# Attention, a gated layer and a soft mixture of experts in one kernel: whole rows for the second matrices, a wider step in the catching-up, and routing in quarter steps

## The chip, the cores and the metric

The kernel runs on one core of a Trainium2 chip. The metric is the device time of one execution in microseconds (us), as the median of several runs. The engines of the core are named as in the profile: PE (TensorE, the matrix engine), DVE (VectorE), ACT (ScalarE), POOL (GpSimd) and SP (SyncE, which here only issues transfers). Data lie in DRAM, in SBUF (128 partitions) and in PSUM, the banks into which PE writes. Transfers go through 16 DMA engines.

## What is computed

Three layers follow each other; the sizes are 4 batches, 8 heads, 576 positions and 64 features per head, so 2304 tokens of 512 features.

```python
# 1: causal attention in a window of 64 positions
scores = scale * np.matmul(q, k.transpose(0, 1, 3, 2))
scores = np.where((rel >= 0) & (rel < 64), scores, -1e9)
x = softmax(scores) @ v                      # as [2304, 512]
# 2: gated layer, d_ff = 1536
x = (x @ w_a) * (x @ w_b) @ w_out            # [2304, 512]
# 3: soft mixture: 8 experts, 4 slots each, F = 1024
logits = x @ phi                             # [2304, 32]
d = softmax(logits, over the tokens)
slot_input = d.T @ x                         # [32, 512]
for e in range(8):
    slot_out[e] = np.maximum(slot_input[e] @ w1[e], 0) @ w2[e]
c = softmax(logits, over the slots)
out = c @ slot_out                           # [2304, 512]
```

The softmax over all tokens is what ties the stages together: no slot input is complete before the last token has been routed, and the experts' matrices (16 MB for w1 and w2 together) can be used only behind that.

## The kernel before

**Tiles and halves.** The tokens are worked in 18 tiles of 128. For each tile, attention gives x; the gated layer is cut into three groups of 512 hidden features (`fg`), and each group into a half `a` (x @ w_a) and a half `b` (x @ w_b), 12 matmuls each in PSUM (`psa`, `psb`, line 454). ScalarE copies psa out, and VectorE multiplies psb with it to g (line 463). These 108 half-blocks are the beat of the kernel. The matrix w_out is never multiplied with each token: its product with phi (`wphi`) makes the logits from g, and the weighted sums of g over the tokens (`ups` at line 600, kept in `acc`) are multiplied with w_out (`wo`) once, at the end.

**What happens between the halves.** A table `events` holds what is issued ahead of, or in the middle of, half-block n; `at(n, f, ...)` enters a step and `run_slot(n)` plays it. Attention steps of later tiles (`att_q`, `att_k`, `att_s`, `att_n`, `att_pt`, `att_pv`, and `load` for q, k, v) stand there, and the routing of earlier ones. Routing of a tile has these steps: `r_b` turns one group of g in 32x32 blocks on VectorE into gq, writes it to DRAM in four transfers `gd` and reads it back as gT in one (lines 486, 492, 497), all issued by SyncE; `r_ul` at half-block `R[t]` makes the sums of tile t-1 and the logits of tile t (`ups` at line 600 and at line 513, then `lt` at line 533 and the softmax); `r_k` and `r_d` follow. `R[t]` is 5 half-blocks behind the tile's last half, but at least 3 behind `R[t-1]`; the start of the kernel (the first five tiles' gated layer, half-blocks 0 to 29) goes without routing, so that from half-block 30 on the routing catches up, one tile every 3 half-blocks: tiles 2 to 9 at 37, 40, 43, 46, 49, 52, 58, 64. gT has four buffers in the pool p3. The queue of PE is the order of the code there (`manual_schedule`); on the other engines a scheduler orders.

**The last tiles.** The last three tiles (`LAST`) take PE to turn g (`r_t`: `tg`, line 138), and the table at the end of the events places their steps in half-block steps. Behind them come `tu` and `xs` (w_out with the sums, slot inputs), `sps`, and the experts: `h` with w1 (line 958), relu, transposes, then `ops` with w2 (line 992). `ops` is worked in two column halves n of 256 and two halves u of the experts (0 to 3, 4 to 7), each in eight steps m of 128 rows. Copies `o`, `so` (line 1010), `sor` (lines 1018 and 1019) prepare the slot outputs of a column half for `tokens_out(n, j)`: two matmuls `op` (line 1032) into a bank, a copy `ob` (line 1039) and a transfer of 256 KB to the output (line 1040). Nine such steps make a column half.

**Prefetching the matrices.** `order` lists the pieces that are wanted: 12 of wo, 64 of w1, 128 half pieces of w2 (`order2`: first all of column half 0, then of 1). `slots` lists the SBUF tiles that come free towards the end (of attention, x, g, and of w_a and w_b), and `fetch` issues for each freed slot as many pieces as it holds, on SyncE (line 748); a transfer waits on SyncE until the tile's last reader is done.

## Time and profile before

| | before |
|---|---|
| median of 3 runs | 518.61 us (518.32 to 519.11) |
| the profiled execution, its own time | 522.32 us |
| its span in the profile | 520.5 us |
| PE busy | 487.2 us, 94% |
| PE's share of the chain that ended last | 78% |
| DVE's share of that chain | 11% |
| moved by the DMA engines | 116.51 MB, mean 224 GB/s |

The span is what lies between the first and the last instruction; the profiled execution's own time has what lies around it. The profile's clock column is the granted share of PE's full clock: 1.00 is 2.4 GHz, 0.50 is 1.2 GHz. A wait in square brackets behind an instruction is idle time of its engine just before it, with what ended it; x is how many instructions a line puts together.

### The profile page before, as it was taken

To read this page: it belongs to the slowest core of one execution; us is meant where nothing else is said; L and a number is where in the kernel's file an instruction comes from. 1 tells how busy PE (TensorE), PEld (TensorE's weight loads), DVE (VectorE), ACT (ScalarE), POOL (GpSimd) and SP (SyncE) were. 2 spreads that over 40 slices of the span, in tenths; PEclk is the share of its full clock that TensorE was granted. 3 is DMA by queue.
4 is the path that set the end of the run, shared out by engine and by line. 5 is a ranking of instruction groups with operands and counts; after the bars stand their busy time and mean duration, and the time that the engine had idled before them with its cause. 6 is when DMAs were issued, how large, how long until landed. Compare 5 with 4: busy or idle time off the path is not lost.

```text
span 520.5 us, 10707 instructions
## 1 busy us (share of the span) xinstructions
PE 487.2 (94%) x4047; PEld 362.3 (70%) x4047; DVE 297.8 (57%) x765; ACT 195.9 (38%) x583; POOL 65.8 (13%) x136
## 2 busy tenths in 40 slices
PE   4769999999999999999899999999999999989993
PEld 2547786778778786877678788787877777743452
DVE  4997897889236757575546637467763210351222
ACT  4886675654314424242323324234432112241022
POOL 4100110100000111111202031131231000020000
PEclk9797999999999999999899999999999999999998
DMA  9999966642136877877885776667689999899997
GB/s 257 281 258 285 296 176 224 224 141 82 42 66 153 199 185 186 213 174 199 205 213 149 169 198 152 183 162 213 164 210 295 345 387 333 293 350 348 350 331 262
DMA packets 143715, 116.51 MB, mean 224 GB/s; under 512 B 81840, under 2 KB 124336, under 8 KB 143664
## 3 DMA queue, kind: packets, MB, share of 16 engines
...
## 4 chain that ended last, share of the span: by engine, by line
PE 78%; DVE 11%; DMA 7%; issue 1%; ACT 1%; SPq 0%; POOL 0%; POOLq 0%; ACTq 0%; DVEq 0%
PE psa L454 26%; PE psb L454 26%; PE xps L364 3%; DMA wo_dram<-wo 3%; PE ops L992 3%; PE s L273 3%; PE h L958 3%; PE ups L600 2%; PE ups L513 2%; PE tk L138 1%; PE tg L138 1%; DVE w L395 1%; DMA ldk<-in_k_dram 1%; PE tq L138 1%; DVE wo L395 1%
## 5 line engine op out<-in xcount | busy, mean ns | idle before, releaser
L454 PE MATMUL psa<-wa,x 128*128 128x512 f32 x648 | 167.3, 402 | 0.2 <-DVE wa L438 0.2
L454 PE MATMUL psb<-wb,x 128*128 128x512 f32 x648 | 165.2, 398 | 0.7 <-DVE wb L438 0.7
L454 PEld LDWEIGHTS psa<-wa,x 128*128 128x128 f32 x648 | 118.8, 190 | 28.0 <-issue 2.8
L454 PEld LDWEIGHTS psb<-wb,x 128*128 128x128 f32 x648 | 118.0, 188 | 26.7 <-issue 2.0
L463 DVE TENSOR_TENSOR g<-psb,g 128x512 f32<-128x512 f32 x53 | 36.5, 689 | 78.2 <-PE psb L454 69.3
L461 ACT COPY g<-psa 128x512 f32<-128x512 f32 x53 | 31.1, 587 | 94.0 <-PE psa L454 90.0
L293 ACT ACTIVATE pr<-pr,nmx 128x128 f32<-128x128 f32 x96 | 37.2, 389 | 17.1 <-DVE nmx L286 17.1
L330 POOL DMA_DIRECT2D pd<-pq x44 | 24.2, 557 | 102.2 <-DVE pq L323 73.8
L486 DVE STREAM_TRANSPOSE gq<-g 128x512 f32<-128x512 f32 x42 | 29.6, 706 | 0.7 <-DMA pd<-pq 0.4
L367 ACT CAST x<-xps 128x512 fp32r<-128x512 f32 x18 | 10.6, 586 | 44.8 <-PE xps L364 44.8
L314 DVE TENSOR_TENSOR pr<-pr,rs 128x512 f32<-128x512 f32 x36 | 24.4, 687 | 0.9
L273 PE MATMUL s<-kTs,qTs 64*64 64x128 f32 x576 | 21.8, 292 | 0.0
L236 POOL COPY kTs<-kTs 128x256 f32<-128x256 f32 x17 | 8.6, 506 | 103.7 <-DVE kTs L247 72.2
L336 POOL DMA_DIRECT2D pT<-pd x22 | 16.6, 757 | 39.2 <-DMA pd<-pq 31.8
L273 PEld LDWEIGHTS s<-kTs,qTs 64*64 64x64 f32 x576 | 17.1, 143 | 5.9 <-issue 4.5
L228 ACT ACTIVATE qTs<-tq 128x512 f32<-128x512 f32 x18 | 10.8, 599 | 26.6 <-PE tq L138 26.5
L138 PE MATMUL tq<-ident,ldq 128*128 128x128 f32 x72 | 11.9, 291 | 9.0 <-DMA ldq<-in_q_dram 7.9
L286 DVE CUSTOM_DVE_ANT_0 pr<-s,masks 128x128 f32<-128x128 f32 x80 | 17.5, 285 | 3.1 <-PE s L273 3.1
L293 ACT ACTIVATE pr<-s,nmx 128x128 f32<-128x128 f32 x48 | 17.1, 375 | 2.4 <-DVE nmx L283 2.4
L293 ACT ACTIVATION_READ_ACCUMULATOR pr<-pr,nmx 128x1 f32 x96 | 17.9, 187 | 0.0
L369 DVE TENSOR_TENSOR x<-xps,x 128x512 fp32r<-128x512 f32 x18 | 12.4, 690 | 8.7 <-ACT x L367 8.7
L549 ACT ACTIVATE e<-lt,nm 128x128 f32<-128x128 f32 x17 | 6.3, 369 | 29.5 <-DVE nm L545 29.4
...
## 6 DMA issues: line engine op xcount, KB each, us to landing
...
```

The source lines that it names most:

```text
L138: nc.tensor.transpose(o, i, ident)
L273: nc.tensor.matmul(sps[h][c, u], lhsT=qT[r, u, c], rhs=kTs[r, t % 2, u, W * b:W * b + P], start=not early, stop=not early or u == 3,)
L286: nc.vector.tensor_tensor_reduce(out=pr[:, u].rearrange("p (a k) -> p a k", a=2), in0=sps[h][:, u].rearrange("p (a k) -> p a k", a=2), in1 ...
L293: nc.scalar.activation(out=pr[:, u], in_=sps[h][:, u] if early else pr[:, u], func=ACTF.Exp, scale=-1.0, bias=nmx[:, i:i + 1], accum_out=s ...
L314: nc.vector.tensor_tensor(out=pr, in0=pr, in1=rs.to_broadcast([P, 4, P]), op=ALU.mult)
L330: nc.gpsimd.dma_start(out=pd[:, :, i].rearrange("j k e -> k j e"), in_=pq[32 * i:32 * i + 32].rearrange("p j h u q -> p j (h u q)"),)
L336: nc.gpsimd.dma_start(out=pT, in_=pd[:, :, :, P * h:P * h + P].rearrange("j k i e -> (j k) i e"))
L364: nc.tensor.matmul(o, lhsT=vt[:, 2 * u + h, :], rhs=r)
L454: nc.tensor.matmul(ps, lhsT=l[:, kk], rhs=r, start=(n == 0), stop=(n == 3 * KD - 1))
L461: nc.scalar.copy(out=pas[t, fg], in_=ps)
L463: nc.vector.tensor_tensor(out=g, in0=ps, in1=pas.pop((t, fg)), op=ALU.mult)
L486: nc.vector.transpose(out=gq.rearrange("p (j c t) -> p c j t", j=4, c=4), in_=gts[t][:, 512 * fg:512 * fg + 512].rearrange("p (c j f) -> p ...
```

## The change

1. **w2 in whole rows.** For experts 0 to 5 (`WHOLE = 6`) a piece of w2 is 128 whole rows of 512 columns, of which partition p holds rows 4p to 4p+3 of a block of 512 rows; neighbouring pieces that land in one slot go in one transfer, so that a partition's part of it is 2, 4 or 6 KB in one run (before: 1 KB runs of half rows). Such a piece is used in both column halves and is held until the second. Experts 6 and 7 stay in column halves. The order of loading is wo, w1 with two pieces of wo moved in among it, experts 0 to 3, experts 4 and 5, then experts 6 and 7 for column half 0 and for column half 1. The relu copies reorder h to match.
2. **Catching up.** `R[t]` is at least 4 behind `R[t-1]` for t from 3 on: tiles 2 to 9 at 37, 41, 45, 49, 53, 57, 61, 65; the `r_b` of a tile stand correspondingly earlier ahead of it. The pool's tag "e" becomes gq with four buffers and pq with one.
3. **Last tiles' routing.** The events table has quarter steps there; the last g is evacuated in two parts, the last transposes on ScalarE and VectorE, the last g is multiplied in two parts, the last tile's sums update acc in one instruction and not in three, the softmax over the slots of the last three tiles is one step, `both` and `turn_c` stand earlier, and the order on ScalarE and VectorE is that of the code from `tu` to the slot inputs.
4. **The end.** The first column half's nine `tokens_out` all stand within the second half's `ops`: four in u = 0, five in u = 1. Before, six stood in u = 0, one right behind u = 1's last `ops`, two behind `so`.

```diff
...
-    N_EX1 = 3
+    N_EX1 = 4
     N_EX2 = 6
-    EARLY = 6
-    PARTS = ((0, 256), (256, 256))
+    WHOLE = 6
+    EARLY = 4
+    HALF = DM // 2
...
-    wbufs = {"w0": 4, "w1": 4, "w2": 2, "w3": 2, "e": N_EX1}
+    wbufs = {"w0": 4, "w1": 4, "w2": 2, "w3": 2, "gq": N_EX1, "pq": 1}
...
-            nc.vector.tensor_tensor(out=g, in0=ps, in1=pas.pop((t, fg)), op=ALU.mult)
+            pa = pas.pop((t, fg))
+            step = 256 if (t, fg) == (NTILE - 1, NFG - 1) else 512
+            for c in range(0, 512, step):
+                nc.vector.tensor_tensor(out=g[:, c:c + step], in0=ps[:, c:c + step], in1=pa[:, c:c + step], op=ALU.mult)
...
+    def r_th(t, fg):
+        gT = pools["p3"].tile([P, 4, P], F32, tag=turn("gT"), name="gT", bufs=2)
+        for h in range(2):
+            tp = ps_t.tile([P, 2, P], F32, tag="t", name="tg")
+            for i in range(2):
+                f = 512 * fg + P * (2 * h + i)
+                transpose(tp[:, i], gts[t][:, f:f + P])
+            if h == 0:
+                nc.scalar.copy(out=gT[:, 0:2], in_=tp)
+            else:
+                nc.vector.tensor_copy(gT[:, 2:4], tp)
+        rst[t, fg] = gT
...
+        rsum = small.tile([P, NLAST], F32, tag="rsum", name="rsum")[:, 0:n]
+        for i in range(n):
+            nc.scalar.activation(
+                out=ce[:, i], in_=lk[:, NS * i:NS * i + NS], func=ACTF.Exp, bias=rm[:, i:i + 1], accum_out=rsum[:, i:i + 1]
+            )
...
+            nc.vector.tensor_tensor(out=cst[:, t:t + n], in0=ce, in1=rr.to_broadcast([P, n, NS]), op=ALU.mult)
...
-    slot_halves = {"g": 3, "as1": 1, "as2": 1, "gT1": 1, "w0": 4, "w1": 4, "w2": 4, "w3": 4}
...
-    order = [("o", c) for c in range(DFF // P)]
-    order += [("1", u, kk, e, n) for u in range(2) for kk in range(KD) for e in range(4) for n in range(2)]
-    order2 = [
-        ("2", n, u, mh, e)
-        for n, (_, nw) in enumerate(PARTS) for u in range(2) for mq in range(MF * nw // 1024)
-        for e in range(4) for mh in (2 * mq, 2 * mq + 1)
-    ]
-    order += order2
+    slot_halves = {"g": 3, "as1": 1, "as2": 1, "gT1": 1, "gq": 1, "w0": 4, "w1": 4, "w2": 4, "w3": 4}
+
+    order = [("o", 0, c) for c in range(DFF // P)]
+    order += [("1", (u, kk, e), n) for u in range(2) for kk in range(KD) for e in range(4) for n in range(2)]
+    for o, n in ((10, 25), (11, 28)):
+        order.insert(n, ("o", 0, o))
+        del order[order.index(("o", 0, o))]
+    order += [("r", (h, e), c) for h in range(2) for e in range(4) for c in range(4)]
+    order += [("r", (h, e), c) for h in range(2) for e in range(4, WHOLE) for c in range(4)]
+    order += [("c", (n, h, e), c) for n in range(2) for h in range(2) for e in range(WHOLE, NE) for c in range(4)]
...
+    def source(key, n):
+
+        kind, which, i = key
+        if kind == "o":
+            return wo_dram[P * i:P * (i + n)].rearrange("(c p) d -> p c d", p=P)
+        if kind == "1":
+            u, kk, e = which
+            return moe2_w1[4 * u + e][P * kk:P * kk + P, 512 * i:512 * (i + n)].rearrange("p (c d) -> p c d", d=512)
+        *n0, h, e = which
+        c = slice(HALF * n0[0], HALF * n0[0] + HALF) if n0 else slice(0, DM)
+        return moe2_w2[e][512 * h:512 * h + 512].rearrange("(p c) d -> p c d", c=4)[:, i:i + n, c]
...
+                w = HALF if key[0] == "c" else 512
+                if key[0] == "1" and nh > 1 and at0 + 2 * w > 512 * nh:
+                    break
+                m = 0
+                while at0 + w * (m + 1) <= 512 * nh and order[nxt[0]:nxt[0] + 1] == [(*key[:2], key[2] + m)]:
+                    k = order[nxt[0]]
+                    exw[k] = x[:, at0 + w * m:at0 + w * (m + 1)]
+                    held[i].append(k)
+                    nxt[0] += 1
+                    m += 1
+                if m == 0:
+                    break
                 nc.sync.dma_start(
-                    out=x[:, 512 * h:512 * (h + nh2)].rearrange("p (c d) -> p c d", d=ncol),
-                    in_=src[r0:r0 + nr, c0:c0 + ncol].rearrange("(c p) d -> p c d", p=P),
+                    out=x[:, at0:at0 + w * m].rearrange("p (c d) -> p c d", d=w), in_=source(key, m)
...
-        events[round(2 * n)].append((f, a))
+        events[round(4 * n) if n > NSLOT - 3 else 2 * round(2 * n)].append((f, a))
...
-        R[t] = max(R[t], R[t - 1] + (3 if t > 1 else 5))
+        R[t] = max(R[t], R[t - 1] + {1: 5, 2: 3}.get(t, 4))
...
-                    at(max(done[t, fg] + 1, r - ((7, 5, 4) if r >= SPLIT + 12 else (4, 3.5, 3))[fg], SPLIT), r_b, t, fg)
+                    at(max(done[t, fg] + 1, r - {3: (4, 3.5, 3), 4: (5, 4, 3.5)}.get(r - R[t - 1], (7, 5, 4) if t > 1 else (4, 3.5, 3))[fg], SPLIT), r_b, t, fg)
...
-        (-1.5, r_t, a, 2), (-1, r_l, a, (2,)), (-.5, r_k, a), (-.5, r_t, b, 2),
-        (0, r_d, a), (0, r_l, b, (2,)), (0, r_t, c, 2), (0, r_u, a), (1, r_k, b), (1, both, 0, "gT0"),
-        (2, r_l, c, (2,)), (3, r_k, c), (3, r_d, b), (3, both, 4, "gT0"), (3, r_u, b),
-        (4, r_d, c), (4, turn_c, 0, (ps_ab, "a")), (4, both, 8, "gT0"), (5, r_u, c), (5, turn_c, 4, (ps_ab, "b")),
+        (-6, both, 0, (None, "as0")), (-5, both, 4, (None, "as0")),
+        (-1.5, r_t, a, 2), (-1, r_l, a, (2,)), (-.75, r_k, a), (-.75, r_t, b, 2), (-.25, r_d, a), (-.25, r_l, b, (2,)),
+        (0, r_u, a), (0, r_th, c, 2), (.25, r_k, b), (.25, turn_c, 0, (ps_ab, "a")), (.25, both, 8, "gT0"), (.5, r_l, c, (2,)),
+        (.5, turn_c, 4, (ps_ab, "b")), (.75, r_k, c), (.75, r_d, b), (.75, r_u, b), (.75, both, 12, "gT0"),
+        (1, r_d, c), (1, turn_c, 8, (ps_t, "x")), (1.5, r_u, c),
...
-        slots.extend([(ex1, "e")] * N_EX1 + [(exs["ex2"], "y")] * N_EX2 + [(gp, "g")] * 2 + [(xp, "x")])
+        slots.extend([(ex1, "gq")] * N_EX1 + [(ex1, "pq")] + [(exs["ex2"], "y")] * N_EX2 + [(gp, "g")] * 2 + [(xp, "x")])
...
-        for f, a in events[2 * n]:
-            run(f, *a)
         pieces = iter(glu(*halves[n], "ab"[n % 2]) if n < NSLOT else ())
-        for _ in range(KD // 2):
+        for kk in range(KD):
+            for f, a in events[4 * n + kk]:
+                run(f, *a)
             next(pieces, None)
-        for f, a in events[2 * n + 1]:
-            run(f, *a)
...
+    with tc.manual_schedule(engines=MANUAL | {mybir.EngineType.Activation, mybir.EngineType.DVE}):
+        cc = r_c(NTILE - NLAST)
+        next(cc)
...
+        nc.vector.tensor_copy(uT[:, 0:2], tus[0])
+        nc.scalar.copy(out=uT[:, 2:MJ], in_=tus[1][:, 0:MJ - 2])
+        turn_c(12, (ps_s, "s1"))
...
+        run(lambda: cc)
         fetch(len(slots))
-        both(12, "gT0")
-        turn_c(12, (ps_s, "s0"))
...
-            nc.vector.tensor_scalar(out=x4[:, c], in0=xps[:, c], scalar1=dr, scalar2=None, op0=ALU.mult)
+            if h:
+                nc.scalar.activation(out=x4[:, c], in_=xps[:, c], func=ACTF.Copy, scale=dr)
+            else:
+                nc.vector.tensor_scalar(out=x4[:, c], in0=xps[:, c], scalar1=dr, scalar2=None, op0=ALU.mult)
...
+        sps = ps_t.tile([P, KD, NS], F32, tag="t", name="sps")
+        turn_c(NTILE - NLAST, (ps_t, "t"))
...
+            hi = hps[c].rearrange("p (f i) -> p i f", i=4)
+            ho = hs.rearrange("p (i f) -> p i f", i=4)
             if c == 0:
-                nc.scalar.activation(out=hs, in_=hps[c], func=ACTF.Relu)
+                nc.scalar.activation(out=ho, in_=hi, func=ACTF.Relu)
             else:
-                nc.vector.tensor_scalar(out=hs, in0=hps[c], scalar1=0.0, scalar2=None, op0=ALU.max)
+                nc.vector.tensor_scalar(out=ho, in0=hi, scalar1=0.0, scalar2=None, op0=ALU.max)
...
+    def w2(e, m, n):
+        h, c = m // 4, m % 4
+        if e >= WHOLE:
+            return use(("c", (n, h, e), c))
+        return (use if n else exw.get)(("r", (h, e), c))[:, HALF * n:HALF * n + HALF]
...
+        if i % 4 == 0:
+            tag = ("w2", "w2", "w1", "w1", "w3")[i // 4]
+            obs[0] = wp.tile([P, 4, 2, HALF], F32, tag=tag, name="ob", bufs=wbufs[tag])
+        ob = obs[0][:, i % 4]
...
-    NOUT = NTILE * DM // (len(PARTS) * 512)
-    slots_out(0, 0, range(MF))
-    slots_keep(0, 0)
     with tc.manual_schedule(engines=MANUAL):
-        slots_out(0, 1, range(MF))
-        slots_keep(0, 1)
-        slots_split(0)
-        slots_out(1, 0, range(MF - EARLY))
-        for j in range(EARLY):
-            slots_out(1, 0, range(MF - EARLY + j, MF - EARLY + j + 1))
-            tokens_out(0, j)
-        slots_keep(1, 0)
-        slots_out(1, 1, range(MF))
-        tokens_out(0, EARLY)
-        slots_keep(1, 1)
-        slots_split(1)
-        for j in range(EARLY + 1, NOUT):
-            tokens_out(0, j)
-        for j in range(NOUT):
-            tokens_out(1, j)
+        for n in range(2):
+            os = {}
+            so = (ps_m, ps_t)[n].tile([P, HALF], F32, tag="mx"[n], name="so", bufs=1)
+            for u in range(2):
+                op = ps_s.tile([P, HALF], F32, tag=f"s{u}", name="ops")
+                for m in range(MF):
+                    slots_out(op, u, m, n)
+                    if n and u and m < NTILE // 2 - EARLY:
+                        tokens_out(0, EARLY + m, sor)
+                    if n and not u and m >= MF - EARLY:
+                        tokens_out(0, m - MF + EARLY, sor)
+                for c in range(0, HALF, P):
+                    os[u, c] = p2.tile([P, P], F32, tag="l4", name="o", bufs=3)
+                    nc.vector.tensor_copy(os[u, c], op[:, c:c + P])
+                    for v in range(2 if u else 0):
+                        pick(so[:, c:c + P], v, os[v, c])
+            sor = split(so)
+        for j in range(NTILE // 2):
+            tokens_out(1, j, sor)
...
```

How the order moves, first on PE in the catching-up: from the sums (`ups<-g,dt`) and logits (`ups<-gT,wphi`) at `R[3]`, which is 40 before and 41 now, to the next sums. A psa or psb row of six matmuls is half of a half-block. Before:

```order
L600 MATMUL ups<-g,dt 32x384 x4
L513 MATMUL ups<-gT,wphi 32x128 x12
L454 MATMUL psa<-wa_1201,x 128x512 x6
L454 MATMUL psa<-wa_1291,x 128x512 x6
L533 MATMUL lt<-l_2238,ri 128x128
L535 MATMUL lt<-ri,l_2238 128x32
L454 MATMUL psb<-wb_1384,x 128x512 x6
L454 MATMUL psb<-wb_1361,x 128x512 x6
L138 MATMUL dps<-ident,e 128x128
L454 MATMUL psa<-wa_443,x 128x512 x6
L454 MATMUL psa<-wa_567,x 128x512 x6
L600 MATMUL ups<-g,dt 32x384 x4
```

Now:

```order
L633 MATMUL ups<-g,dt 32x384 x4
L530 MATMUL ups<-gT,wphi 32x128 x12
L455 MATMUL psb<-wb_1384,x 128x512 x6
L455 MATMUL psb<-wb_1361,x 128x512 x6
L455 MATMUL psa<-wa_443,x 128x512 x6
L550 MATMUL lt<-l_2237,ri 128x128
L552 MATMUL lt<-ri,l_2237 128x32
L455 MATMUL psa<-wa_567,x 128x512 x6
L455 MATMUL psb<-wb_182,x 128x512 x6
L139 MATMUL dps<-ident,e 128x128
...
L633 MATMUL ups<-g,dt 32x384 x4
```

Between the sums stand three half-blocks before and four now (the last ones are left out); `lt` stands one half-block behind the logits before, one and a half now.

Second, SyncE's queue at the last loads, from the two slots that the last half of the gated layer sets free. Here xw is the slot that is filled (with its number), 128x1024 is a whole-row piece of 4 KB per partition, 128x4x256 four column-half pieces. Before:

```order
L748 DMA xw_5184<-in_moe2_w1_dram 128x1024 x2
L748 DMA xw_5187<-in_moe2_w2_dram 128x4x256 x2
L748 DMA xw_5304<-in_moe2_w2_dram 128x4x256
L748 DMA xw_5306<-in_moe2_w2_dram 128x4x256
L748 DMA xw_5308<-in_moe2_w2_dram 128x4x256
L748 DMA xw_5308<-in_moe2_w2_dram 128x2x256
L748 DMA xw_5311<-in_moe2_w2_dram 128x2x256
```

Now:

```order
L782 DMA xw_5201<-in_moe2_w1_dram 128x1024 x2
L782 DMA xw_5204<-in_moe2_w1_dram 128x1024
L782 DMA xw_5204<-in_moe2_w2_dram 128x1024
L782 DMA xw_5332<-in_moe2_w2_dram 128x1024
...
L782 DMA xw_5435<-in_moe2_w2_dram 128x1536
L782 DMA xw_5435<-in_moe2_w2_dram 128x512
L782 DMA xw_5438<-in_moe2_w2_dram 128x1536
L782 DMA xw_5438<-in_moe2_w2_dram 128x2x256
L782 DMA xw_5449<-in_moe2_w2_dram 128x2x256
```

The second of these slots takes a further piece of w1 and then the first of w2, where it took w2 alone; column-half pieces come only at the end.

Third, PE in the routing of the last tiles, from the last half-block (b of tile 17) on; the first `tg` in it is tile 16's, the second tile 17's. Before:

```order
L454 MATMUL psb<-wb_1384,x 128x512 x6
L533 MATMUL lt<-l_4830,ri 128x128
L138 MATMUL tg<-ident,g 128x128 x4
L454 MATMUL psb<-wb_1361,x 128x512 x6
L138 MATMUL dps<-ident,e 128x128
L513 MATMUL lps<-gT,wphi 32x128 x4
L138 MATMUL tg<-ident,g 128x128 x4
L600 MATMUL ups<-g,dt 32x384 x4
```

Now:

```order
L455 MATMUL psb<-wb_1384,x 128x512 x3
L550 MATMUL lt<-l_4834,ri 128x128
L139 MATMUL tg<-ident,g 128x128 x4
L455 MATMUL psb<-wb_1384,x 128x512 x3
L455 MATMUL psb<-wb_1361,x 128x512 x3
L139 MATMUL dps<-ident,e 128x128
L530 MATMUL lps<-gT,wphi 32x128 x4
L455 MATMUL psb<-wb_1361,x 128x512 x3
L633 MATMUL ups<-g,dt 32x384 x4
L139 MATMUL tg<-ident,g 128x128 x4
```

The last half-block's twelve matmuls are cut in four where they were cut in two: `lt` and the `tg` of tile 16 stand a quarter earlier in it, `dps` and the logits `lps` inside it, and the sums of tile 15 (`ups`) ahead of tile 17's `tg`.

## Rows read from the trace of the kernel before

**Rows 1.** The page's engines: busy us, share of the span, instructions

```profile
PE 487.2 (94%) x4047; PEld 362.3 (70%) x4047; DVE 297.8 (57%) x765; ACT 195.9 (38%) x583; POOL 65.8 (13%) x136
```

**Rows 2.** Busy time by stretch: stretch, length, engines (instructions), clock, DMA share, GB/s

```profile
254.00:400.00 146.00, 146.00 (x1241) 117.06 (x1240) 85.84 (x290) 49.70 (x182) 31.79 (x60) 1.00 0.73 188
...
456.00:464.00 8.00, 6.34 (x47) 2.92 (x51) 3.89 (x17) 2.14 (x10) 2.99 (x10) 1.00 1.07 351
464.00:504.00 40.00, 39.77 (x424) 17.87 (x420) 10.04 (x30) 7.07 (x20) 0.88 (x3) 1.00 1.10 350
```

**Rows 3.** PE's waits, 130 to 400 us: sum, count, longest

```profile
PE ups L513 <- DMA gT<-gd: 3.3, 2, 2.7
PE lt L533 <- DVE acc L611: 0.7, 1, 0.7
```

**Rows 4.** Timeline of PE: start, length, instruction, count, wait

```profile
222.65 3.04 PE L454 MATMUL psa<-wa,x 128*128 128x512 f32 x12
...
232.35 0.84 PE L513 MATMUL ups<-gT,wphi 128*32 128x128 f32 x24
...
249.10 0.58 PE L513 MATMUL ups<-gT,wphi 128*32 128x128 f32 x8 [2.66 <-DMA gT<-gd]
249.60 4.43 PE L454 MATMUL psa<-wa,x 128*128 128x512 f32 x12
```

**Rows 5.** Busy time in the stretch behind the longest wait

```profile
249.24:252.65 3.41, 3.41 (x15) 2.49 (x10) 3.03 (x7) 0.36 (x2) 0.67 (x2) 0.50 1.04 237
```

**Rows 6.** Timeline of SyncE's queue ahead of that wait

```profile
233.24 1.36 SPq L208 DMA_DIRECT2D lda<-in_v_dram  x2
234.64 1.43 SPq L208 DMA_DIRECT2D ldb<-in_v_dram  x1
...
242.81 0.34 SPq L497 DMA_DIRECT2D gT<-gd  x1
...
246.13 0.34 SPq L497 DMA_DIRECT2D gT<-gd  x1
```

**Rows 7.** Busy time in three stretches with prefetching

```profile
400.00:404.00 4.00, 4.00 (x46) 2.78 (x45) 0.81 (x2) 1.17 (x2) 0.00 (x0) 1.00 0.99 348
...
420.00:428.00 8.00, 8.00 (x44) 6.36 (x43) 1.68 (x3) 1.08 (x2) 0.00 (x0) 1.00 1.02 417
...
464.00:474.00 10.00, 9.77 (x86) 4.12 (x82) 2.70 (x15) 3.74 (x14) 0.88 (x3) 1.00 1.10 348
```

**Rows 8.** Waits of SyncE's queue from 400 us on

```profile
SPq L748 <- PE lt L533: 4.9, 1, 4.9
```

**Rows 9.** Timeline of SyncE's queue, the outputs

```profile
498.10 18.67 SPq L1040 DMA_DIRECT2D out_dram<-ob  x18
```

**Rows 10.** The tile ob, its transfers

```profile
DMA to landing us min/median/max: 2.2/3.2/7.1
```

**Rows 11.** Timeline of PE from 436 us on

```profile
450.66 0.60 PE L138 MATMUL tg<-ident,g 128*128 128x128 f32 x4
...
467.61 2.76 PE L958 MATMUL h<-xw,sinT 128*32 128x512 f32 x18 [0.15 <-DVE rsum L577]
...
487.10 7.11 PE L992 MATMUL ops<-xw,hT 128*32 128x256 f32 x126
...
496.91 0.50 PE L1032 MATMUL op<-sor,cT 128*128 128x256 f32 x2
...
497.91 0.50 PE L1032 MATMUL op<-sor,cT 128*128 128x256 f32 x2
...
502.36 3.66 PE L992 MATMUL ops<-xw,hT 128*32 128x256 f32 x64
...
509.54 2.83 PE L1032 MATMUL op<-sor,cT 128*128 128x256 f32 x16 [1.10 <-DVE sor L1019]
```

**Rows 12.** Timeline of VectorE at the end

```profile
496.05 0.43 DVE L1019 TENSOR_TENSOR sor<-so,sor 64x256 fp32r<-64x256 f32 x1 [1.09 <-ACT sor L1018]
...
506.09 0.69 DVE L1039 COPY ob<-op 128x512 f32<-128x512 f32 x1 [3.54 <-PE ops L992]
```

More of the change, by code (lines that the diff above doesn't have):

```diff
@@ L483, in r_b @@
     def r_b(t, fg):
-        gq = pools["ex1"].tile([P, 512], F32, tag="e", name="gq")
+        gq = pools["ex1"].tile([P, 512], F32, tag="gq", name="gq")
         nc.vector.transpose(
@@ L586, in r_d @@
         dt = p2.tile([P, P], F32, tag="dt", name="dt", bufs=1)
-        nc.vector.tensor_copy(dt, dps)
+        if t < NTILE - 2:
+            nc.vector.tensor_copy(dt, dps)
+        else:
+            nc.scalar.copy(out=dt, in_=dps)
         rst[t, "d"] = dt
@@ L607, in r_u @@
             co = rst.pop((t, "co"))
-            step = P if t == NTILE - 1 else FJ
-            for c in range(0, FJ, step):
-                h = acc[:, c:c + step]
-                nc.vector.scalar_tensor_tensor(
-                    out=h, in0=h, scalar=co, in1=ups[:, c:c + step], op0=ALU.mult, op1=ALU.add
-                )
+            nc.vector.scalar_tensor_tensor(out=acc, in0=acc, scalar=co, in1=ups, op0=ALU.mult, op1=ALU.add)
     def r_ul(t):
@@ L673, in turn_c @@
         c, n = c4s.pop(t0)
-        cp = bank[0].tile([P, 4, P], F32, tag=bank[1], name="cp")
+        cp = bank[0].tile([P, 4, P], F32, tag=bank[1], name="cp", bufs=2 if bank[1] == "t" else 1)
         for i in range(n):
@@ L914, in swa_glu_softmoe_kernel @@
     nc.vector.reciprocal(out=dr, in_=dn)
-    tp = ps_t.tile([P, MJ, P], F32, tag="t", name="tu")
     uT = exs["ex2"].tile([P, MJ, P], F32, tag="as0", name="uT", bufs=2)
@@ L918, in swa_glu_softmoe_kernel @@
     x4 = exs["ex2"].tile([P, DM], F32, tag="as0", name="x4", bufs=2)
-    sps = ps_t.tile([P, KD, NS], F32, tag="x", name="sps", bufs=1)
-    with tc.manual_schedule(engines=MANUAL):
+    with tc.manual_schedule(engines=MANUAL | {mybir.EngineType.Activation, mybir.EngineType.DVE}):
+        cc = r_c(NTILE - NLAST)
+        next(cc)
+        tus = [ps_t.tile([P, 2, P], F32, tag="t", name="tu") for _ in range(2)]
         for m in range(MJ):
-            transpose(tp[:, m], acc[:, P * m:P * m + P])
-            nc.vector.tensor_copy(uT[:, m], tp[:, m])
-        turn_c(8, (ps_t, "t"))
+            transpose(tus[m // 2][:, m % 2], acc[:, P * m:P * m + P])
+        nc.vector.tensor_copy(uT[:, 0:2], tus[0])
+        nc.scalar.copy(out=uT[:, 2:MJ], in_=tus[1][:, 0:MJ - 2])
+        turn_c(12, (ps_s, "s1"))
         for m in range(MJ):
@@ L979, in swa_glu_softmoe_kernel @@
         hTs.append(hT)
-    sos = {}
-    ops = {}
-    os = {}
-    def slots_out(n, u, ms):
-        nw = PARTS[n][1]
-        nm = 512 // nw
-        if ms[0] == 0:
-            ops[n, u] = ps_s.tile([P, nw], F32, tag=f"s{u}", name="ops")
-        for m in ms:
-            for e in range(4):
-                nc.tensor.matmul(
-                    ops[n, u][32 * e:32 * e + 32], lhsT=hTs[u][m // 4][:, m % 4, 32 * e:32 * e + 32],
-                    rhs=use(("2", n, u, m // nm, e))[:, nw * (m % nm):nw * (m % nm) + nw],
-                    start=(m == 0), stop=(m == MF - 1),
-                )
@@ L1010, in slots_pick, with slots_out @@
+    def slots_out(op, u, m, n):
+        for e in range(4):
             nc.tensor.matmul(
-                sos[n][:, c:c + P], lhsT=exs["sel"][:, u].rearrange("p a s -> p (a s)"), rhs=os[n, u, c],
-                start=(u == 0), stop=(u == 1),
-            )
-    def slots_split(n):
-        so, nw = sos[n], PARTS[n][1]
-        sor = exs["ex2"].tile([P, nw], F32R, tag="as0", name="sor", bufs=2)
+                op[32 * e:32 * e + 32], lhsT=hTs[u][m // 4][:, m % 4, 32 * e:32 * e + 32], rhs=w2(4 * u + e, m, n),
+                start=(m == 0), stop=(m == MF - 1),
+            )
@@ L1018, in slots_split, with pick, split @@
+    def pick(so, u, o):
+        nc.tensor.matmul(
+            so, lhsT=exs["sel"][:, u].rearrange("p a s -> p (a s)"), rhs=o, start=(u == 0), stop=(u == 1)
+        )
+    def split(so):
+        sor = exs["ex2"].tile([P, HALF], F32R, tag="as0", name="sor", bufs=2)
         nc.scalar.copy(out=sor, in_=so)
         nc.vector.tensor_tensor(out=sor[W:P], in0=so[W:P], in1=sor[W:P].bitcast(F32), op=ALU.subtract)
-        sos[n] = sor
+        return sor
+    banks = ((ps_ab, "a"), (ps_ab, "b"), (ps_t, "t"), (ps_t, "t"))
```

123 lines of the change are left out of this document (45 added, 78 removed).

## The prediction

> **What bounds the kernel now.** I read the page first, then a table by stage, then who waits in each stage. TensorE (PE) is busy for 94% of the span, VectorE for 57%, ScalarE for 38% [rows 1]: PE's work sets the time, and where PE waits there is time to be had. By stage [rows 2] it is not one limit. From 254 to 400 us PE is busy throughout. From 456 to 464 us, in the routing of the last tiles, it is busy 6.34 of 8.00 us. From 464 to 504 us it is busy 39.77 of 40.00 us while the DMA engines stand at a share of 1.10: two limits lie on top of each other there, and taking away one gives little. Who makes PE wait between 130 and 400 us is a short list [rows 3]: 3.3 us for gT in two pieces, 0.7 us for acc in one. So there are three places: those waits, the last routing, and the end behind the second matrices.
>
> **Catching up, 4 half-blocks instead of 3.** The large piece of the wait for gT, 2.66 us, stands ahead of the ups matmul at 249.10 us [rows 4]. Behind it the granted clock is 0.50 for 3.41 us [rows 5] (and 1.00 from 254 us on [rows 2]): that level is 1.2 and not 2.4 GHz, and twelve matmuls of psa take 4.43 us where they took 3.04 [rows 4]: 1.4 us more. Sum: 3.3 + 0.7 + 1.4 = 5.4 us. The cause is SyncE's queue [rows 6]: between the sums and logits matmuls of r_ul of tile 6 (232.35) and the landing of tile 7's third gT (issued at 246.13, PE released at 249.10) three value loads were issued, and gd and gT alternate, each gT waiting for the gd just ahead of it. p3 has four gT buffers, so the second and third gT of a tile go only after the tile before was used: this turn-round, 249.10 - 232.35 = 16.8 us, has to fit between two r_ul. Half-blocks with attention in them cost (249.60 - 222.65 - 2.66) / 6 = 4.0 us here, so 3 of them are 12 us and 4 are 16. In the new order the gq transposes of a tile's last third stand 5 to 7 half-blocks ahead of their use on VectorE (3.5 at most before), and at most two loads fall into a turn-round. Without the loads (1.36 + 1.43 us of issue) and with two steps of the kind from 242.81 to 246.13, 3.3 us each, and 3 us of landing, it is some 10 us: it fits into 16. I take 0.3 us left over: **-5.1 us**; ends -5.4, and -1.3 if a wait of the large kind stays. The gq and pq tags come to five buffers where the old tag had three, so no transpose waits for a buffer that it did not wait for before: 0.
>
> **The second matrices.** Before, the column halves are loaded one after the other, in 1 KB rows: 256 KB (262,144 bytes) take 0.75 us at the 348 to 351 GB/s that the DMA engines hold [rows 7]. 4 KB rows (the first matrices) run at 417 GB/s: 0.63 to 0.64 us. Of rows of 2 KB alone the nearest stretch has 348 GB/s at share 0.99, with other traffic before and behind it. Now 48 of the 64 pieces of 256 KB are whole rows: 32 of them in pieces of 4 or 6 KB, 16 alone in 2 KB, and for these I take the middle of 0.63 and 0.75, 0.67: 32 x 0.64 + 16 x 0.67 = 31.2 us for 48 x 0.75 = 36.0. That is **4.7** us off the stream (ends: 5.8 and 0). Against it, two halves of the x and g slots stay empty because two chunks of wo now split pairs, so that one more 512 KB piece of the first matrices stands behind the release at 450.6 us (SyncE waits 4.9 us for it [rows 8]): at 417 GB/s 1.26 us: **+1.3**. The last weight of before lands at some 498.10 + 7.1 - 0.7 = 504.5 us: the first output, issued at 498.10 [rows 9], stands behind the weights and must be the one that took 7.1 us [rows 10], and 0.7 is its own time; now at 504.5 + 1.3 - 4.7 = 501.1.
>
> But the order of need changes, and that decides the tail. The first column half used to need 32 pieces; now it needs all 48 of whole rows and 8 narrow ones, since the rows of experts 4 and 5 and the narrow pieces of 6 and 7 come last. The 56th lands 8 x 0.75 before the end, at 495.1; the release comes 0.5 us later (a tg group of 0.60 us [rows 11] now stands ahead of it): 495.6. Half of one u is left then, 32 of the 126 instructions of 7.11 us [rows 11]: 1.8 us, so the first column half ends at 497.4 and not at 494.2 (487.10 + 7.11): **+3.2 us**. PE gets to the second u at 490.7 (midway in the same 126), less what the routing saves, and sits idle until the 52nd piece, 492.6. Idle time of 2.66 us cost 1.4 us of clock above; here I take **+1.0** (ends 0, no fall, and 1.8: 32 matmuls at half the rate). The second column half has eight narrow pieces left to wait for, and lands as the forecast of the last weight says, 501.1 + 0.5; PE passes it about there, since its 128 instructions of that half take 7.2 us from 499.8.
>
> The Trainium skill speaks against this part: its page DMA: Bandwidth & Descriptors (Specifications) has transfers of 512 B and more at line rate. By that, 1 KB rows leave nothing to gain, and the 4.7 us would be 0; rows 7 have 417 against 349 GB/s. That is rival B below.
>
> **Routing in quarter steps.** The chain from the release at 450.66 to the first h matmul (467.61) takes 17 us [rows 11]. Two-part evacuation, one softmax for three tiles, uT and x4 shared by two engines and c4 ahead of the h phase take between nothing (if the fixed order on ScalarE and VectorE makes them wait for each other) and 3 us off, most likely PE's idle time there, 8.00 - 6.34 = 1.7 [rows 2]. All of it ends in the wait for the stream: **0**. If the stream were early, it would be worth its 1.7. The two `both` that go ahead of the last halves cost ScalarE and GpSimd nothing that PE waits for (ScalarE: 38% [rows 1]). The copies of hps, that now read PSUM with a stride of four elements, cost between 0 and twice the 0.69 us that a copy of this size takes [rows 12], in front of the same wait: 0.
>
> **The end.** Nine tokens_out now stand ahead of the last ops matmul, six before. One of them adds 0.55 us there: with one in each step, steps go from 496.91 to 497.91, 1.00 us, and the eight ops matmuls of a step alone are 7.11 / 126 x 8 = 0.45 [rows 11]. 3 x 0.55 = **+1.65**. Behind it, from the last ops (502.36 + 3.66) to the first op of the second half (509.54) went 3.5 us [rows 11], with the evacuation of o behind a copy of ob that holds VectorE from 506.09 for 0.69 us [rows 12]. Without copies in between it takes what the first half took, from 494.2 to sor's end at 496.48 [rows 12] and 0.1 for the step to PE: 2.4. That is -1.1, and the queue of evacuations behind it is three copies shorter: **-1.35** in all (ends -0.7 and -2.0). The nine last outputs then go as fast as they do now: 0.
>
> **Sum:** -5.1 + 3.2 + 1.0 + 1.65 - 1.35 = -0.6 us. The span was 520.5 and would be 519.9. The profiled execution took 522.3 us with what lies around the span, the median of the runs 518.6; I take the difference over as it is: **518.0 us**, its own range 516.5 to 519.5. A measurement of this kernel tells some 0.2%, 1.0 us, from no change.
>
> **Rivals.** (A) *The stream arrives at its best rows and the clock stays*: all wide pieces at 417 GB/s (-1.0), no clock lost (-1.0), the release not later (-0.5): 515.5. For it: 420 to 428 us holds 417 with nothing disturbing. Against it: pieces that begin in the middle of a slot go out singly in 2 KB rows. (B) *Wide rows are no faster*: at 349 GB/s the 4.7 us are gone and come on top at the same place, PE's wait in the first column half: 522.7. It turns from same to slower once the 12.6 MB take over 32.8 us (384 GB/s). For it: the 348 GB/s at 2 KB, and each partition now steps 8 KB between its pieces; against it: the 417. By the page of the Trainium skill named above this would be the outcome; the trace's 417 GB/s speaks against it. (C) *One large wait for gT stays* in the catching-up, moved to another tile: 518.0 + 2.66 + 1.4 - 0.3 = 521.8; it decides where the third gT lands over 4 half-blocks, 16 us, after the r_ul before. The lead of gq speaks against it.
>
> **Chances.** Forecast 0.50, A 0.22, B 0.13, C 0.08, the rest 0.07 to both sides, mostly slower. Below 517.6, 0.2% less than the median, lie A and a third of the forecast: faster 0.41. Same: 0.31. Slower than 519.6: B, C, most of the rest and the forecast's edge: 0.28. The range reaches from below A's time into the range between forecast and B: 515.2 to 521.3.
>
> **What would show it.** Step 1: no wait for gT over 0.5 us and no clock of 0.50 between 190 and 260 us; r_ul of tile 7 later than tile 6 by four half-blocks. Step 2: whole rows at about 400 GB/s, and PE idle for 3 to 5 us ahead of the second u of the first column half with the DMA as releaser; if PE does not wait there, A. Step 3: clock of 0.50 there. Step 4: the last ops matmul ends at some 506.8 us (506.02 - 5.1 + 3.2 + 1.0 + 1.65), the span some 13 us behind it, where it was 14.5 (520.5 - 506.02). Wrong would be: a stream that has slots to wait for between the xs and the h matmuls, or new waits on ScalarE in the routing that last over 4 us.

## The result, and the profile after

The changed kernel takes **524.58 us** (median of 6 runs, 523.78 to 525.07), the kernel before 518.86 us (median of 6, 518.01 to 522.15): a ratio of 1.0091, with a 95% interval of 1.0066 to 1.0117. It is slower, by 5.7 us of the medians. The forecast was 518.0 us in a range of 515.2 to 521.3; the time lies above the range.

The profiled execution of after took 524.17 us, its span 522.4. Its engines, its chain by engine, its costliest group of the tail with the idle time before it, and (last line) the only waits of PE between 130 and 430 us, two of 0.3 us:

```profile
PE 489.7 (94%) x4047; PEld 361.7 (69%) x4047; DVE 297.6 (57%) x753; ACT 193.7 (37%) x586; POOL 65.5 (13%) x136
...
PE 77%; DMA 11%; DVE 7%; ACT 2%; issue 1%; SPq 0%; DVEq 0%
...
L1022 PE MATMUL ops<-xw,hT 128*32 128x256 f32 x256 | 19.9, 414 | 5.6 <-DMA xw<-in_moe_w_dram 5.6
```

```profile
PE dps L139 <- ACT ce L600: 0.6, 2, 0.3
```

The waits of [rows 3] are gone. What came in their place stands in the tail: 5.6 us of idle time ahead of `ops`, ended by the weights' transfers, and 11% of the chain on the DMA engines where it was 7%. The timeline of PE there (start, length, instruction, count, wait), which answers to [rows 11]:

```profile
461.98 7.07 PE L989 MATMUL h<-xw,sinT 128*32 128x512 f32 x64 [0.38 <-DVE sinT L980]
...
478.81 0.62 PE L1022 MATMUL ops<-xw,hT 128*32 128x256 f32 x2
...
479.94 4.07 PE L1022 MATMUL ops<-xw,hT 128*32 128x256 f32 x66
488.46 1.06 PE L1022 MATMUL ops<-xw,hT 128*32 128x256 f32 x2 [4.45 <-DMA xw<-in_moe_w_dram]
490.71 5.17 PE L1022 MATMUL ops<-xw,hT 128*32 128x256 f32 x58 [1.19 <-DMA xw<-in_moe_w_dram]
495.81 1.39 PE L1029 MATMUL so<-o,sel 128*128 128x128 f32 x8
...
507.88 1.50 PE L1022 MATMUL ops<-xw,hT 128*32 128x256 f32 x24
...
511.66 3.08 PE L1048 MATMUL op<-sor,cT 128*128 128x256 f32 x18 [0.92 <-DVE sor L1036]
```

PE gets through 68 `ops` of the first column half, stops at the second u, and does the last 58 in 5.17 us. In [rows 11] 126 of them took 7.11 us, so 58 should take 3.3. The busy time by stretch (length, engines, clock, DMA share, GB/s) shows the stream and the clock there:

```profile
478.00:484.00 6.00, 6.00 (x79) 3.17 (x76) 2.27 (x5) 0.17 (x1) 0.00 (x0) 1.00 1.04 418
484.00:488.50 4.50, 0.06 (x2) 0.04 (x2) 0.20 (x1) 0.00 (x0) 0.00 (x0) 0.83 1.05 358
488.50:492.00 3.50, 2.31 (x16) 0.74 (x20) 0.00 (x0) 0.00 (x0) 0.00 (x0) 0.50 1.10 347
492.00:496.00 4.00, 4.00 (x51) 1.96 (x44) 0.08 (x1) 0.00 (x0) 0.00 (x0) 0.77 1.10 349
```

Whole rows arrive at up to 418 GB/s, column halves at 347 to 349. PE idles until 488.46 us, and the granted clock is 0.50 (1.2 GHz) from 487.01 to 493.84 us.

### The profile page after: what moved, and what is told of

Same layout as the page of the kernel before. It is cut to its first block, busy times and chain, and to the rows that moved or that the text cites. A ratio compares the mean times of both kernels' runs of the same rounds, so it can differ in the third digit from the quotient of the medians.

```text
span 522.4 us, 10689 instructions
## 1 busy us (share of the span) xinstructions
PE 489.7 (94%) x4047; PEld 361.7 (69%) x4047; DVE 297.6 (57%) x753; ACT 193.7 (37%) x586; POOL 65.5 (13%) x136
## 4 chain that ended last, share of the span: by engine, by line
PE 77%; DMA 11%; DVE 7%; ACT 2%; issue 1%; SPq 0%; DVEq 0%
PE psb L455 27%; PE psa L455 25%; DMA xw<-in_moe_w_dram 6%; PE xps L365 3%; DMA wo_dram<-wo 3%; PE s L274 3%; PE ups L633 3%; PE ops L1022 3%; PE ups L530 2%; PE tk L139 1%; PE op L1048 1%; PE tg L139 1%; PE tq L139 1%; PE tp L139 1%; PE two L139 1%
## 5 line engine op out<-in xcount | busy, mean ns | idle before, releaser
L455 PE MATMUL psb<-wb,x 128*128 128x512 f32 x648 | 167.1, 400 | 1.8 <-DVE g L467 1.4
L455 PEld LDWEIGHTS psa<-wa,x 128*128 128x128 f32 x648 | 117.5, 188 | 26.5 <-issue 3.2
L467 DVE TENSOR_TENSOR g<-psb,g 128x512 f32<-128x512 f32 (+1 forms) x54 | 36.6, 679 | 69.8 <-PE psb L455 61.6
L1022 PE MATMUL ops<-xw,hT 128*32 128x256 f32 x256 | 19.9, 414 | 5.6 <-DMA xw<-in_moe_w_dram 5.6
```

The lines of the kernel that those rows point to most:

```text
L455: nc.tensor.matmul(ps, lhsT=l[:, kk], rhs=r, start=(n == 0), stop=(n == 3 * KD - 1))
L467: nc.vector.tensor_tensor(out=g[:, c:c + step], in0=ps[:, c:c + step], in1=pa[:, c:c + step], op=ALU.mult)
L1022: nc.tensor.matmul(op[32 * e:32 * e + 32], lhsT=hTs[u][m // 4][:, m % 4, 32 * e:32 * e + 32], rhs=w2(4 * u + e, m, n), start=(m == 0), sto ...
```

## Experiments

Three theories were on the table. **T1**: the profiled execution of before was not a typical one; its waits for gT are rare, so removing them gains little in the median. **T2**: the waits are there every time, and the loss elsewhere is larger than forecast. **T3**, beside either: the first column half waits because 56 of the 64 pieces of w2 (of 256 KB) must land before it can end, and all of the stream's delay counts there.

**A second profile of before**, nothing edited.

> The kernel before, unchanged, looked at a second time. Theory 1: the profiled execution of before (522.32 us, 3.5 us over the median of 518.86) held a wait for gT that most executions do not have; then a second profile near the median shows no wait of 2.66 us ahead of the ups matmuls around 249 us and no stretch with a granted clock of 0.50 behind it, sum of PE's waits for gT and acc between 130 and 400 us under 1.5 us, span 516 to 518. Theory 2: the wait is in every execution; then it is there again with 3.3 us for gT, and the execution's own time is above the median because of something around the span.

519.93 us against 518.76 for the runs of before beside it (ratio 1.002, 0.9997 to 1.0043: the same kernel); its profiled execution 518.73 us, span 516.9, 3.6 us less than the one shown ahead. PE's waits from 130 to 430 us, and the timeline at the place of [rows 4]:

```profile
PE lt L533 <- DVE acc L611: 1.4, 2, 1.2
PE xps L364 <- DMA pT<-pd: 0.9, 2, 0.7
```

```profile
244.34 0.85 PE L600 MATMUL ups<-g,dt 128*32 128x384 f32 x8
245.01 0.84 PE L513 MATMUL ups<-gT,wphi 128*32 128x128 f32 x24
245.78 3.02 PE L454 MATMUL psa<-wa,x 128*128 128x512 f32 x12
...
482.22 7.11 PE L992 MATMUL ops<-xw,hT 128*32 128x256 f32 x126
...
497.48 4.96 PE L992 MATMUL ops<-xw,hT 128*32 128x256 f32 x64
...
505.94 2.83 PE L1032 MATMUL op<-sor,cT 128*128 128x256 f32 x16 [1.10 <-DVE sor L1019]
```

The ups matmuls run as one group of 24, without a wait, and psa behind them at full clock in 3.02 us. The wait for gT is not in every execution, as T1 has it. (It also shows the stream as a limit of before: the last 64 `ops` take 4.96 us where the first execution took 3.66.)

The order on SyncE's queue is the same in both executions, the three value loads included (at 228.88 and 230.22 us in this one), and so it does not make the wait by itself. Here the third gT of tile 7 landed at 244.43 us, 14.2 us behind the logits matmuls of tile 6 (230.25), just ahead of PE's matmuls at 245.01. In the execution shown ahead it took 16.7 us, to 249.05, and PE wanted it at 246.44. The delay was there before the value loads: a `gd` issued at 228.25 us took 4.47 us to land, its counterpart here (225.61) 2.61 us, and the gT behind it was issued 0.5 us behind tile 6's matmuls, not 1.9 us ahead of them. What slowed that transfer is open.

**The catching-up undone in after:**

```diff
-        R[t] = max(R[t], R[t - 1] + {1: 5, 2: 3}.get(t, 4))
+        R[t] = max(R[t], R[t - 1] + (3 if t > 1 else 5))
...
-   r - {3: (4, 3.5, 3), 4: (5, 4, 3.5)}.get(r - R[t - 1], (7, 5, 4) if t > 1 else (4, 3.5, 3))[fg]
+   r - ((7, 5, 4) if r >= SPLIT + 12 else (4, 3.5, 3))[fg]
```

> The kernel after with the catching-up undone: R[t] 3 half-blocks behind R[t-1] and the block transposes where they were before, all else as after. Theory 1 (the wait is in few executions of before): 524.5 us, at most 1.0 us from after. Theory 2 (the wait is in every execution, its removal was worth 4 to 5 us and the loss elsewhere is that much larger): 528 to 529 us, with the wait for gT back in the profile.

524.53 us, as after and not the 528 of T2; the ratio to before is 1.0135 (1.0109 to 1.0162), that of after 1.0091. PE's waits in this execution were 2.4 us for acc and none over 0.2 us for gT:

```profile
PE lt L550 <- DVE acc L641: 2.4, 1, 2.4
```

In this profile the stretch with the catching-up is 3.0 us longer than in after, but the first column half is 1.3 us shorter (A and E in the table below). So the run speaks against T2, and the catching-up itself is sized by the next one.

**The catching-up alone, in before:** the same lines the other way round, with the tags gq and pq.

> The kernel before with the catching-up of after alone: R[t] 4 behind R[t-1], the block transposes earlier, the tags gq and pq. The forecast's sum had -5.1 us for it. By the second look at before, in which the gT wait is 0.1 us and the only waits of the catching-up are 1.4 us for acc, it is worth at most 1.5 us: 517 to 519 us, within 0.3% of before. If the wait for gT were frequent: 514 to 515.

518.09 against 519.07 us (0.9983, 0.9961 to 1.0005): 0.9 us by the ratio (from 2.0 us faster to 0.3 slower), not told apart from nothing. The forecast had 5.1. T1 holds.

**Fewer whole rows**, `WHOLE = 4`:

> The kernel after with WHOLE = 4: only experts 0 to 3 in whole rows, experts 4 to 7 in column halves. Theory of the order of need: the first column half needs 48 of 64 pieces of 256 KB and not 56, its last piece lands some 4.9 us earlier (488.8 and not 493.7), the two waits of PE there (4.45 and 1.19 us) shrink to 0 to 1 us and the stretch at clock 0.50 behind them goes; the last weight lands 1.3 us later (500.6), which nobody waits for; 516 to 518.5 us, 6 to 8 under after. Rival, the stream's rate is what counts: 1.3 us slower than after, 526.

519.0 us (1.0005 of before, 0.9982 to 1.0028), 5.6 under after; its waits in the first column half were 1.65, 0.28 and 0.14 us, and the clock was 1.00 throughout:

```profile
478.39 6.14 PE L1022 MATMUL ops<-xw,hT 128*32 128x256 f32 x98
484.82 0.62 PE L1022 MATMUL ops<-xw,hT 128*32 128x256 f32 x2 [0.28 <-DMA xw<-in_moe_w_dram]
487.09 1.91 PE L1022 MATMUL ops<-xw,hT 128*32 128x256 f32 x26 [1.65 <-DMA xw<-in_moe_w_dram]
```

The expected 518.5 at most was missed by half a microsecond; the theory's direction held, and its waits, at 2.07 us in sum, were longer than the 0 to 1 expected.

**No whole rows**, `WHOLE = 0`, the order as before:

```diff
-    order += [("r", (h, e), c) for h in range(2) for e in range(4) for c in range(4)]
-    order += [("r", (h, e), c) for h in range(2) for e in range(4, WHOLE) for c in range(4)]
-    order += [("c", (n, h, e), c) for n in range(2) for h in range(2) for e in range(WHOLE, NE) for c in range(4)]
+    order += [("c", (n, h, 4 * u + e), c) for n in range(2) for u in range(2) for h in range(2) for e in range(4) for c in range(4)]
```

> The kernel after with WHOLE = 0: all of w2 in column halves, first those of column half 0 (experts 0 to 3, then 4 to 7), as the order was before; routing, catching-up and end as after. Theory of the order of need: no wait in the first column half, its ops end at 486 to 487 us; the last weight lands 2.5 to 4 us later than in after (502 to 503), and the second half's ops end some 1.5 us behind that, 504; the end 13 us behind it: span 516.5 to 517.5, 518 to 519.5 us. Rival, the routing and the end of after cost the time and not the rows: within 1.5 us of after, 524.5.

518.51 us (1.0011, 0.9989 to 1.0033), as expected. The waits are now in the second column half, and the stream runs at the slow rate all the time (timeline of PE; busy time of a stretch):

```profile
495.72 0.62 PE L1020 MATMUL ops<-xw,hT 128*32 128x256 f32 x2 [1.34 <-DMA xw<-in_moe_w_dram]
...
501.53 0.62 PE L1020 MATMUL ops<-xw,hT 128*32 128x256 f32 x2 [1.19 <-DMA xw<-in_moe_w_dram]
```

```profile
464.00:472.00 8.00, 8.00 (x66) 2.56 (x62) 1.98 (x3) 0.60 (x1) 0.00 (x0) 1.00 1.09 348
```

So the routing and the end of after cost nothing; the time was lost in how w2 is loaded, its rows and their order.

**Slots filled as before:** wo in front, pairs of w1 split where half a slot is left, `WHOLE = 6`.

```diff
-    for o, n in ((10, 25), (11, 28)):
-        order.insert(n, ("o", 0, o))
-        del order[order.index(("o", 0, o))]
...
-                if key[0] == "1" and nh > 1 and at0 + 2 * w > 512 * nh:
-                    break
```

> The kernel after with the chunks of wo all in front, and pairs of w1 split where a slot has one half left, as before: no slot half stays empty, and one piece of w1 of 512 KB less stands behind the release at the last half-block. By the forecast's term (+1.3 us) the last weight lands 1.3 us sooner behind that release (51.0 instead of 52.3 us, or 49.8 instead of 51.07), the first column half ends as much sooner, and the time is 523.2. If the stream behind the release is set by something else: 524.5.

**519.86 us** (1.0014, 0.9992 to 1.0037): 4.7 us under after, where 1.3 was expected. What is called the release below is the issue of the first transfer that waited for the last half-blocks. The last weight landed 49.96 us behind the release (445.76 and 495.72 us), against 52.32 in the first profile of after (446.96 and 499.28). PE's wait is 2.76 us and not 5.6:

```profile
478.74 4.07 PE L1017 MATMUL ops<-xw,hT 128*32 128x256 f32 x66
...
485.57 6.08 PE L1017 MATMUL ops<-xw,hT 128*32 128x256 f32 x60 [2.76 <-DMA xw<-in_moe_w_dram]
```

**A second profile of after**, nothing edited, to tell chance from the kernel:

> The kernel after, unchanged, looked at a second time beside the kernel before. By the sum over stages from the first look (against the second look at before: catching-up -1.1, last half-blocks +0.7, routing and h -3.5, first column half +8.8, second +0.4, end -1.4 us) it is 4 us slower than before, with the waits of 4 to 6 us and the clock of 0.50 in the first column half; the 1.6 us that the first look had at the start (the 48th half-block at 159.43 and not 157.83 us) is chance of one execution: 522.5 to 523.5 us. If that start belongs to the kernel after: 524.5 again, and the 48th half-block at 159.4.

524.72 us (1.0107, 1.008 to 1.0135): neither 523.5 nor a late start (the half-block was at 158.41). This execution lost more in the first column half:

```profile
488.31 1.06 PE L1022 MATMUL ops<-xw,hT 128*32 128x256 f32 x2 [5.33 <-DMA xw<-in_moe_w_dram]
...
490.57 5.48 PE L1022 MATMUL ops<-xw,hT 128*32 128x256 f32 x58 [1.20 <-DMA xw<-in_moe_w_dram]
```

Its last weight came 53.29 us behind the release. Two stretches of this execution, and below them the same two of the kernel with the slots filled as before (busy time; the last three columns are clock, DMA share, GB/s):

```profile
450.00:454.00 4.00, 3.65 (x36) 1.76 (x36) 2.05 (x9) 1.99 (x9) 1.65 (x6) 1.00 0.83 264
466.00:470.00 4.00, 4.00 (x30) 1.36 (x22) 1.29 (x2) 0.60 (x1) 0.00 (x0) 1.00 0.95 331
```

```profile
450.00:454.00 4.00, 3.65 (x37) 1.79 (x29) 1.89 (x9) 1.99 (x9) 1.49 (x5) 1.00 0.93 328
466.00:470.00 4.00, 4.00 (x32) 1.32 (x25) 1.29 (x2) 0.60 (x1) 0.00 (x0) 1.00 1.04 397
```

There the stream falls below its rate, though transfers are issued and have not landed: 4 us at 64 and at 66 GB/s less are 0.26 MB each, some 0.65 us each at 400 GB/s. Why is not settled; the first profile of after has 318 GB/s in the first of these stretches, close to the 328 here.

**Between the two orders:** slots filled as before, with `WHOLE` = 4, 3 and 2, for the latter two the column halves in order of experts 0 to 3, then 4 to 7.

> As e6_pairs_split, with WHOLE = 4. Against WHOLE = 4 with the moved wo (519.0 us, waits of 1.65 and 0.28 us in the first column half, last weight 53.5 us behind the release): stream 1.3 us earlier, waits under 0.8 us, 517 to 518.

> As e6_pairs_split, with WHOLE = 3 and the column-half pieces in order of experts 0 to 3, then 4 to 7, within each column half. The first column half needs 44 of 64 pieces. Theory of the order of need: no wait over 0.3 us in the first column half, its ops take 8.3 to 9 us; the last weight lands 53 us behind the release, the second half ends 2.5 us behind that: span 514 to 515.5, time 1 to 2.5 us under the 519.0 of WHOLE = 4. Rival, the last weight rules now: as WHOLE = 4, 519.

> As e7_whole_3_pairs_split, with WHOLE = 2: the other flank. The first column half needs 40 of 64 pieces and doesn't wait in WHOLE = 3 already; 8 more pieces in column halves put the last weight 0.7 us later, and the second column half waits for it: 515 to 516.5 us, 0.3 to 1 us over WHOLE = 3. If even fewer whole rows help: 514.

`WHOLE = 4`: **515.09 us** (0.9929, 0.9902 to 0.9955), two below the 517 expected. `WHOLE = 3`: **515.01 us** (0.9933, 0.9906 to 0.996), inside. `WHOLE = 2`: 516.7 us (0.9961, 0.9937 to 0.9985), 0.2 over the range. With 4 the `ops` of the first column half still stretch, with 3 they take what they took before the change:

```profile
478.67 7.87 PE L1017 MATMUL ops<-xw,hT 128*32 128x256 f32 x126
```

```profile
478.07 7.11 PE L1017 MATMUL ops<-xw,hT 128*32 128x256 f32 x126
```

Both beat the kernel before by 0.7% and after by 1.8%. `WHOLE = 4` with and without the moved pieces of wo (519.0 and 515.09 us) is also a second pair for the filling of the slots: 3.9 us.

No run has `WHOLE = 0` with the slots filled as before. What whole rows are worth apart from the routing and the end is therefore not told by a time, only by the stream's rate.

## The time by stage

Lengths in us, worked out from the timelines of PE. A: from the half-block b at 157.83 us (second profile of before; the same one in each) to the last group of 18 psb at 437.57. B: from there to the end of the last psb. C: to the first `h`. D: to the first `ops`. E: to the last `ops` of the first column half, F: of the second. G: to the end of the span.

| kernel | A | B | C | D | E | F | G | sum |
|---|---|---|---|---|---|---|---|---|
| before, the execution shown ahead | 282.51 | 10.21 | 14.95 | 18.36 | 8.24 | 11.82 | 14.52 | 360.61 |
| before, second profile | 279.75 | 10.21 | 14.96 | 18.34 | 8.24 | 13.12 | 14.49 | 359.11 |
| before, catching-up alone | 278.60 | 10.21 | 15.10 | 18.35 | 8.25 | 12.03 | 14.32 | 356.86 |
| after | 278.61 | 10.94 | 12.99 | 16.83 | 17.07 | 13.51 | 13.00 | 362.95 |
| after, second profile | 278.61 | 10.93 | 12.99 | 16.83 | 18.27 | 13.49 | 12.98 | 364.10 |
| after, catching-up undone | 281.57 | 10.95 | 12.99 | 16.83 | 15.82 | 13.50 | 12.95 | 364.61 |
| after, WHOLE = 4 | 278.60 | 10.92 | 12.99 | 16.83 | 11.74 | 13.51 | 13.19 | 357.78 |
| after, WHOLE = 0 | 279.04 | 10.93 | 12.99 | 16.84 | 8.24 | 17.38 | 12.89 | 358.31 |
| slots filled as before, WHOLE = 6 | 279.06 | 10.95 | 12.99 | 16.83 | 14.05 | 13.52 | 13.01 | 360.41 |
| the same, WHOLE = 4 | 279.31 | 10.93 | 12.99 | 16.83 | 9.01 | 13.49 | 12.75 | 355.31 |
| the same, WHOLE = 3 | 278.60 | 10.94 | 12.99 | 16.83 | 8.24 | 13.90 | 13.14 | 354.64 |
| the same, WHOLE = 2 | 278.63 | 10.94 | 12.99 | 16.83 | 8.24 | 14.56 | 13.04 | 355.23 |

The second profiles of before and after differ by 5.0 us, the medians by 5.7 and 6.3. E alone takes 10.0; the gain of 3.5 us in C and D, less the 0.7 in B, ends in it. What lies ahead of A takes 157.5 to 160.5 us in these executions, and differs by 2.1 us between the two of before and by 1.0 between the two of after.

## Why the prediction was wrong

**The base, and with it the catching-up: the step that failed.** The waits of [rows 4] are gone in after, and in the profiled pair the stretch A is 282.51 - 278.61 = 3.9 us shorter. But "I take the difference over as it is" put the 5.1 us against a median in which most of them are not. The execution shown ahead took 522.32 us, 3.7 above the median of 518.61: a row of one execution that is 0.7% above the median was the sign. Set against the second profile of before, which is 3.6 us shorter, it loses 2.8 us in A and 2.1 us ahead of A, and gains 1.3 us in F. Ahead of A it has a wait that the second profile lacks:

```profile
PE tk L138 <- DMA ldk<-in_k_dram: 4.4, 1, 4.4
```

In the median the catching-up alone is worth 0.9 us, and at most 2.0 by its interval, where 5.1 was forecast: that is some 4 us of the miss of 6.6, and at least 3.1. On the execution that the sum was made on, the forecast was nearer: a span of 519.9 us where 522.4 was measured, the last `ops` at 506.8 where it was 509.38.

The second profile is no average either: at 518.73 us it lies 1.2 below the median of its own runs. Three profiles with the old step have A at 282.51, 279.75 and 281.57 us, nine with the new one at 278.60 to 279.31. So single executions lose 1 to 4 us to the old step, with different waits (gT, pT and acc, acc alone), and SyncE's queue, which the prediction names as the cause, is the same where the wait for gT is missing. Why the medians keep only 0.9 us of it is not shown.

**The packing of the slots: a term that was mis-sized.** +1.3 us was one piece of 512 KB at full rate, and one piece it is: behind the release 18.35 MB are loaded in after, 17.83 MB with the slots filled as before. The medians of two pairs put 4.7 us (519.86 against 524.58) and 3.9 us (515.09 against 519.0) on it. The last weight shows 2.4 and 3.3 us of this (49.96 behind the release against 52.32 and 53.29), 2.0 with `WHOLE = 4` (51.45 against 53.45), and only 1.1 against the run with the catching-up undone, whose tail is that of after (51.07). The piece itself is 1.3; the stretches in which the stream falls below its rate are the rest of what is seen of the stream, and between executions they vary. What makes them is open. The clock takes a part as well: behind the longer wait it is 0.50 for 6.83 us in after (from 487.01 us), behind the shorter one for 3.41 us (from 486.60); and from the landing of the last piece that the first column half needs to the end of that half go 2.2 us in the one and 1.6 in the other. The sums by stage show 2.5 and 3.7 us of the 4.7; where the rest lies is not shown.

**Whole rows: right.** -4.7 us was expected off the stream. With the slots filled as before the last weight lands 49.96 us behind the release, in the two profiles of before 53.91 and 55.40: -3.9 and -5.4. (The sum itself slips a little: 36.0 - 31.2 is 4.8, and the middle of 0.63 and 0.75 is 0.69 and not 0.67, by which it would be 4.5.) The Trainium skill, in its page DMA: Bandwidth & Descriptors (Specifications), puts line rate at 512 B and more; the trace disagrees, with 348 GB/s at 1 KB and 394 to 418 at 2 to 6 KB outside the stretches just named. So rival B is false, though the sign of the result is the one it forecast; so are A (the first column half did wait) and C (no wait for gT was left in after).

**The order of need: right.** Without the packing term the forecast had the first column half 4.2 - 1.3 = 2.9 us later. From the last psb group to the end of E it is 54.82 us with the slots filled as before, and 51.76 in both profiles of before: +3.1. With the packing it is 57.83 and 59.02, +6.1 and +7.3, where +4.2 was forecast. The agreement of +3.1 with 2.9 holds a small error of the clock's term (below). The series of pieces needed shows the same: E is 14.05, 9.01, 8.24 and 8.24 us for 56, 48, 44 and 40.

**The clock** was forecast at +1.0 (0 to 1.8). The 58 matmuls took 1.9 us more than at full clock, but the 56th piece landed only at about 493.7 us and the column half ended at 495.88, 2.2 us later, where 1.8 had been set for it at full clock: by this estimate some 0.4 us of it is on the path.

**Routing: right in the sum.** C and D are 3.5 us shorter and B 0.7 longer, and all of it ended in the wait for the stream, as said; where the stream is early (`WHOLE` = 3 and 4 with the slots filled as before) the 2.8 us count, and 1.7 was forecast for that case. Of D's 1.5 us nothing was forecast.

**The end: right.** F was to grow by 1.65: 13.51 against 11.82 in the execution shown ahead. G was to shrink by 1.35: 13.00 against 14.52 and 14.49. In the second profile of before F is 13.12, since its last `ops` wait for weights (the last one lands at 501.16 us, 1.3 before they end); against that only 0.4 of F's growth is a loss.

The sum, in the forecast's terms and against the second profile of before: -1.1 (not -5.1), +6.1 to +7.3 up to the end of E (not +4.2), +0.4 (not +1.65), -1.5 (not -1.35): +3.9 to +5.1 us. What lies between that and 5.7 is not told apart from the spread of what lies ahead of A. What was said ahead of the prediction of 16 MB for w1 and w2 together is their size each (16.8 MB); no term rests on it.
